# Attention with hashed masks and a SwiGLU FFN on one core: units 0 and 1 mix their heads, batch 0 is loaded in longer runs, weights are issued at other steps

## The chip, the cores and the metric

The kernel runs on one core of a Trainium2 chip. The metric is the device time of one execution in microseconds; the median of three runs of the kernel before is 370.31 us (369.69 to 371.39). A core has five engines, each with a queue of its own that it works through in order: TensorE (PE; its weight loads are listed as PEld), VectorE (DVE), ScalarE (ACT), GpSimd (POOL) and SyncE (SP). SP, ACT and POOL issue DMAs; sixteen DMA engines carry them out.

## The reference

Attention over 4 batches, 8 heads, 768 tokens, 64 dimensions. A query sees a key when the signs of their six projections agree. The output of the attention, as 3072 rows of 512, goes through an RMS norm and a gated FFN of width 1536.

```python
q_bits = (np.einsum('bhsd,dk->bhsk', q, proj) > 0)     # k likewise, 6 bits
mask = q_bucket[:, :, :, None] == k_bucket[:, :, None, :]
scores = np.where(mask, scale * q @ k.T, -1e9)
attn = np.exp(scores - max); attn = attn / (attn.sum(-1) + 1e-9)
x = (attn @ v).transpose(0, 2, 1, 3).reshape(B * S, H * D)
xn = x / np.sqrt(np.mean(x * x, -1) + 1e-6) * rms_g
g = xn @ w_gate
out = (g * sigmoid(g) * (xn @ w_val)) @ w_out
```

## The kernel before

**Units and steps.** A unit is one batch with one half of its queries (384): 8 units, `u = 2 * batch + half`. A head of a unit takes three steps; a step is two score matmuls of 128 keys x 384 queries (`scores`, L301) and one exp of 128x768 (`probs`, L313), so a unit has 24 steps (`NS`) and the kernel 192. Steps are numbered 0 to 191 here; the code writes them as a window `w` and a step `s` in it, with `at(w, s, f, ...)` entering work in `plan`. The loop at L605 emits, at each step, the scores of the next step, the exp of this one, and then all that the plan has for it. The order of every engine's queue is this order of emission: nothing is scheduled afterwards (`manual_schedule`, L60).

**The mask.** q and k of a head stand transposed in a tile `QK`, 64 rows of fp16 values and below them rows of hash bits, so that one matmul over all rows gives the score plus a large term that is highest where all six bits agree; the bias of the exp (`EBIAS`) takes it away again. Two heads (a pair, `hp`) share 12 bit rows: `select` (L212) multiplies the signs by `sel`, which keeps only the head's own six rows on the k side. With them `QK` has 76 rows (`KROWS`).

**Getting a pair ready.** Loads come into tiles of `lpool` (8 buffers). Batch 0 is turned on PE in float32 (`turn_pe`, L152: three transposes to a PSUM bank, a copy on DVE), batches 1 to 3 on DVE (`turn_dve`, L178). POOL casts the result to fp16 into `QK` (`cast_half` L170, `cast_pool` L187). The hash is a float32 matmul of the turned tile with `pj` (`hash_half`, L195), a sign on DVE (`signs`, L205) and `select`. The bits are then copied into rows 64 and up of `QK`: by DVE for the first two pairs (`hash_direct`, L218), by DMAs on SP's queue for the others (`hash_one` L234, `hash_two` L248). v is cast on POOL (`v_prep`, L267); `v_mean` (L280) gives the small constant term of the denominator's 1e-9.

**Attention out.** `av` (L318) multiplies the probabilities with v into `o_ps`, which has one PSUM buffer for a pair of heads; `attn_out` (L334) divides on DVE (`otmp`, `rcp`) and POOL (`x`, `sq`); `sumsq` reduces the squares on DVE. After the last pair of a unit comes `norm` (L364: DVE, POOL, DVE) and `turn_x` (L379).

**FFN.** `gate` (L390) and `value` (L401) work on 12 tiles of 128 columns; `project` (L415) gives the rows of the output. The FFN of unit u lies in window u+1, its projection in window u+2. The transposed tiles, hash, mean, gate, value, normed x and projection all take their PSUM bank from one pool of three (`gps`, tag "g").

**Weights.** `load_w` (L473) issues each weight matrix in two halves on POOL's queue, cast to fp16 on the way: wg at steps 3 and 7, wv at 11 and 15, wo at 30 and 34 (L531 to L534).

**Batch 0 and unit order.** In batch 0 partition p holds tokens 6p to 6p+5 (`c`). Half 0 of the queries is tokens c = 0 to 2, half 1 c = 3 to 5. A load of q or k goes to a tile `[128, 6, 2, D]` (token, head of the pair, dimension), in runs of 64 floats. Unit 0 runs all its eight heads, then unit 1 all its eight; the q half that only unit 1 needs is loaded late for pairs 0 and 1 (`qlate`). Loads of batch 1 are entered at steps 16, 20, 33 and 38, their turns at 32, 37, 43 and 48 (`spots`, L537).

Of the kernel before, what the change touches and what calls it, by code (L numbers as in the profile page):

```python
# [31 lines left out]
def kernel(  # L32
# [34 lines left out]
    pj = const.tile([128, 32], FP32, name="pj")  # L67
    sel = const.tile([128, 2], FP32, name="sel")
    ebias = const.tile([128, 1], FP32, name="ebias")
# [15 lines left out]
    def natural_tiles(hp):  # L85
        raw[0, hp] = [
            lpool.tile([128, 6, 2, D], FP32, name=n, tag="L") for n in ("qn", "kn")
        ] + [None]

    def load_natural(eng, hp, which, lo=0, hi=6):  # L90
        i = 0 if which == "q" else 1
        for hh in range(2):
            eng.dma_start(
                out=raw[0, hp][i][:, lo:hi, hh],
                in_=(q, k)[i][0, 2 * hp + hh].rearrange("(p c) d -> p c d", c=6)[:, lo:hi],
            )

    def load_v(eng, b, hp):
        vn = lpool.tile([128, 2, 6, D], FP32, name="vn", tag="L")
        for hh in range(2):  # L100
            eng.dma_start(
                out=vn[:, hh],
                in_=v[b, 2 * hp + hh].rearrange("(p c) d -> p c d", c=6),
            )
        raw[b, hp][2] = vn
# [16 lines left out]
    qlate = npool.tile([128, 2, 3, 2, D], FP32, name="qlate")  # L122
    qTlate = npool.tile([128, 2, HALF], FP32, name="qTlate")

    def load_late(eng, hp):
        for hh in range(2):
            eng.dma_start(
                out=qlate[:, hp, :, hh],
                in_=q[0, 2 * hp + hh].rearrange("(p c) d -> p c d", c=6)[:, 3:6],
            )  # L130
# [5 lines left out]
    KROWS = D + 12  # L136
    qT, kT, QK = {}, {}, {}
# [9 lines left out]
    def half_of(hp, which, half):  # L147
        if which == "q" and half == 1 and hp < 2:
            return qTlate[:, hp, :]
        return (qT if which == "q" else kT)[0, hp][:, half * HALF : (half + 1) * HALF]  # L150

    def turn_pe(hp, which, half, act=()):  # L152

        if which == "q" and half == 1 and hp < 2:
            src = qlate[:, hp]
        else:
            src = raw[0, hp][0 if which == "q" else 1][:, 3 * half : 3 * half + 3]
        src = src.rearrange("p c h d -> p c (h d)")
        ps = bank("t_ps", [128, 3, 128])
        for i in range(3):  # L160
            nc.tensor.transpose(ps[:, i, :], src[:, i], ident)  # L161
        psf = ps.rearrange("p c t -> p (c t)")
        nc.vector.tensor_copy(half_of(hp, which, half), psf)
        o = (0 if which == "q" else S) + half * HALF
        for hh in act:
            nc.scalar.copy(
                QK[0, 2 * hp + hh, "h"][0:64, o : o + HALF], psf[64 * hh : 64 * hh + 64, :]
            )

    def cast_half(hp, which, half, heads=(0, 1)):  # L170
        o = (0 if which == "q" else S) + half * HALF
        for hh in heads:
            nc.gpsimd.tensor_copy(
                QK[0, 2 * hp + hh, "h"][0:64, o : o + HALF],
                half_of(hp, which, half)[64 * hh : 64 * hh + 64, :],
            )
# [10 lines left out]
    def cast_pool(b, hp, which):  # L187
        src = (qT if which == "q" else kT)[b, hp]
# [6 lines left out]
    def hash_half(parts):  # L195

        ps = bank("d_ps", [128, HALF])
        for t, src in parts:
            nc.tensor.matmul(  # L199
                ps[32 * t : 32 * t + 32, :], pj, src,  # L200
# [17 lines left out]
    def hash_direct(n, *parts):  # L218
# [275 lines left out]
    def at(w, s, f, *a):  # L494
        if s >= NS and w < 7:
            w, s = w + 1, s - NS
# [117 lines left out]
    for s in range(NS, NS + 6):  # L614
        for f in plan[7, s]:
            f()
# [43 lines left out]
```

## Time and profile before

| what | us |
|---|---|
| median of three runs | 370.31 |
| the profiled execution | 370.79 |
| its span, first to last instruction | 369.0 |
| PE busy | 337.6 (91%) |
| DVE busy | 239.7 (65%) |
| ACT busy | 217.4 (59%) |
| POOL busy | 148.4 (40%) |
| exp (L313), 192 times | 164.8, 0.900 each |
| score matmuls (L301), 384 times | 95.9 |
| exp of step 0, 24, 48 starts at | 10.17, 46.11, 85.44 |
| exp of step 72, 96, 120, 144, 168 starts at | 130.28, 171.95, 212.20, 252.66, 291.62 |
| last exp starts at | 329.69 |

The page gives busy time by engine and by groups of instructions; a line number is a line of the kernel. The view of windows cuts the span into stretches and gives for each the busy time of every engine with the count of instructions, the granted clock of PE as a share of full speed, and the share and rate of the DMA engines. The timeline lists instructions by start and length, with the idle time before them in brackets and what ended it. The chain of waits follows the work that ended last back through what released it. In the DMA view, q0 is the queue of POOL's DMAs (the weights) and q1 that of SP's; a line gives packets, megabytes and the time that the packets took as a share of sixteen engines.

### The profile page before, as it was taken

Reading aid. Unit: us, or ns where it says so; the run is one execution under the profiler, and the core shown is the slowest. Engines: PE = TensorE matmul, PEld = TensorE weight load, DVE = VectorE, ACT = ScalarE, POOL = GpSimd, SP = SyncE. Lnnn points to the kernel's source line nnn. Section 1 sums busy time; section 2 is a strip of 40 time slices with the busy share of each in tenths; the row PEclk is TensorE's granted clock in tenths of the full one; section 3 lists DMA queues with packets and bytes.
Section 4 is the critical chain, followed back from the end, with each engine's and each line's share of the span. In section 5 each row is a group of like instructions: output and inputs, shape, how many; then the busy total and the mean of one; then the engine's idle time right before and its main releaser. Section 6 shows DMA issues by size and latency. Waiting matters only on the chain.

```text
span 369.0 us, 7544 instructions
## 1 busy us (share of the span) xinstructions
PE 337.6 (91%) x2928; PEld 199.0 (54%) x2928; DVE 239.7 (65%) x484; ACT 217.4 (59%) x316; POOL 148.4 (40%) x216
## 2 busy tenths in 40 slices
PE   7685869998989999999999999999999999998995
PEld 3452546554555645655566555555565556664552
DVE  4771748895568965986489727885566545674770
ACT  2552875654557755775667666766577667661321
POOL 3574655635513762772247522851211121112000
PEclk9986998998999999999999999999999999999999
DMA  7998699980858812004889101001100010002002
GB/s 181 213 189 180 106 180 165 167 181 20 179 105 153 170 24 80 11 3 71 169 185 187 26 30 57 3 5 25 47 30 0 2 57 30 3 0 87 0 3 85
DMA packets 100500, 31.42 MB, mean 85 GB/s; under 512 B 89968, under 2 KB 96368, under 8 KB 100464
## 3 DMA queue, kind: packets, MB, share of 16 engines
q1 hardware_dynamic: 96128, 25.82, 31.9%
q0 software_dynamic: 2656, 4.72, 7.8%
q10 hardware_dynamic: 1680, 0.40, 0.5%
q8 instruction: 23, 0.38, 0.5%
q14 instruction: 13, 0.11, 0.1%
HBM read 28.32 MB, written 6.29 MB: 94 GB/s over the span
## 4 chain that ended last, share of the span: by engine, by line
PE 75%; DVE 10%; ACT 9%; DMA 2%; issue 2%; POOL 1%; SPq 0%; DVEq 0%; ACTq 0%
PE y_ps L420 17%; PE g_ps L396 16%; PE s_ps L301 15%; PE v_ps L406 12%; PE o_ps L326 7%; ACT psb L313 7%; PE d_ps L199 4%; DMA QK<-bits 2%; ACT t L398 2%; DVE xnT L385 2%; DVE bits L214 1%; PE x_ps L384 1%; DVE kT L182 1%; PE t_ps L161 1%; DVE a L408 1%
## 5 line engine op out<-in xcount | busy, mean ns | idle before, releaser
L313 ACT ACTIVATE psb<-s_ps,ebias 128x768 f16<-128x768 f32 x192 | 164.8, 900 | 21.8 <-PE s_ps L301 21.7
L301 PE MATMUL s_ps<-QK 76*128 76x384 f16 x384 | 95.9, 332 | 15.9 <-DMA QK<-bits 6.7
L398 ACT ACTIVATE t<-g_ps 128x384 f32<-128x384 f32 x96 | 47.1, 490 | 65.3 <-PE g_ps L396 65.3
L348 POOL TENSOR_TENSOR x<-otmp,rcp 128x384 f32<-128x384 f32 x32 | 26.5, 827 | 140.0 <-DVE rcp L346 140.0
L406 PE MATMUL v_ps<-xnT,wv 128*128 128x384 f16 x384 | 78.6, 327 | 1.7 <-DVE a L408 1.6
L396 PE MATMUL g_ps<-xnT,wg 128*128 128x384 f16 x384 | 78.4, 326 | 1.1 <-DVE xnT L385 1.1
L420 PE MATMUL y_ps<-wo,ht 128*128 128x512 f16 x288 | 70.8, 380 | 0.0
L408 DVE SCALAR_TENSOR_TENSOR a<-t,g_ps 128x384 f32<-128x384 f32 x96 | 52.3, 545 | 23.4 <-ACT t L398 22.2
L301 PEld LDWEIGHTS <-QK 76*128 76x128 f16 x384 | 36.7, 99 | 52.5 <-issue 24.3
L326 PEld LDWEIGHTS <-psb 128*128 128x128 f16 x1152 | 53.2, 98 | 20.1 <-issue 4.1
L409 DVE SCALAR_TENSOR_TENSOR ht<-a,v_ps 128x384 f16<-128x384 f32 x96 | 53.2, 554 | 13.5 <-PE v_ps L406 4.7
L326 PE MATMUL o_ps<-vl,psb 128*128 128x65 f16 x1152 | 58.1, 195 | 0.5 <-ACT psb L313 0.3
L406 PEld LDWEIGHTS <-wv 128*128 128x128 f16 x384 | 34.9, 98 | 23.2 <-issue 4.1
L396 PEld LDWEIGHTS <-wg 128*128 128x128 f16 x384 | 35.1, 97 | 22.1 <-issue 1.6
L427 ACT COPY ysb<-y_ps 128x512 f32<-128x512 f32 x24 | 14.0, 585 | 55.9 <-PE y_ps L420 42.0
L420 PEld LDWEIGHTS <-ht 128*128 128x128 f16 x288 | 26.2, 98 | 25.7 <-issue 1.5
L353 POOL TENSOR_TENSOR sq<-x 128x384 f32<-128x384 f32 x32 | 26.5, 827 | 2.5
L191 POOL CAST QK<-qT 64x768 f16<-64x768 f32 x28 | 23.0, 822 | 10.5 <-DVE qT L182 8.5
L191 POOL CAST QK<-kT 64x768 f16<-64x768 f32 x28 | 23.0, 821 | 8.0 <-DVE kT L182 5.1
L341 DVE TENSOR_TENSOR otmp<-o_ps,cvb 128x390 f32<-128x390 f32 x32 | 17.8, 556 | 12.6 <-PE o_ps L326 12.3
L357 DVE TENSOR_REDUCE ssp<-sq 128x3 f32<-128x384 f32 x32 | 17.1, 534 | 10.8 <-POOL sq L353 10.7
L182 DVE STREAM_TRANSPOSE qT<-qL 128x384 f32<-128x384 f32 x24 | 20.5, 868 | 0.0
(64 smaller groups left out, 228.3 us busy)
## 6 DMA issues: line engine op xcount, KB each, us to landing
vn<-in_v_dram SPq DMA_DIRECT2D x32, 192.0 KB
out_dram<-ysb SPq DMA_DIRECT2D x24, 256.0 KB
qL<-in_q_dram SPq DMA_DIRECT2D x48, 96.0 KB
kL<-in_k_dram SPq DMA_DIRECT2D x48, 96.0 KB
wg<-in_moe_w_gate_dram POOLq DMA_DIRECT2D x2, 768.0 KB, 7.9
wv<-in_moe_w_val_dram POOLq DMA_DIRECT2D x2, 768.0 KB, 7.0
wo<-in_moe_w_out_dram POOLq DMA_DIRECT2D x2, 768.0 KB, 8.9
kn<-in_k_dram SPq DMA_DIRECT2D x6, 192.0 KB
```

Source lines behind the costliest of these rows:

```text
L191: nc.gpsimd.tensor_copy(QK[b, 2 * hp + hh, "h"][0:64, o : o + S], src[64 * hh : 64 * hh + 64, :])
L301: nc.tensor.matmul(ps[:, j, 0:HALF], QK[b, h, "h"][0:KROWS, S + jt * 128 : S + (jt + 1) * 128], QK[b, h, "h"][0:KROWS, half * HALF : (half ...
L313: nc.scalar.activation(psb[u, h][:, 2 * ch : 2 * ch + 2, :], sps.pop((u, i))[:, :, 0:HALF], AF.Exp, bias=ebias, scale=ESCALE,)
L326: nc.tensor.matmul(o[:, c, hh, 0:65], psb[u, h][:, jt, c * 128 : (c + 1) * 128], vls[b % 2][:, h, jt, 0:65], start=(hh == 0 and i == 0), s ...
L348: nc.gpsimd.tensor_mul(xd.rearrange("p c (h d) -> p c h d", h=2), tmp[:, :, :, 0:64], r.to_broadcast([128, 3, 2, 64]),)
L353: nc.gpsimd.tensor_mul(sq, xd, xd)
L396: nc.tensor.matmul(g, wg[:, kt, fs], xnT[u][:, kt, :], start=(kt == 0), stop=(kt == 3))
L398: nc.scalar.activation(t, g, AF.Tanh, scale=0.5)
L406: nc.tensor.matmul(vv, wv[:, kt, fs], xnT[u][:, kt, :], start=(kt == 0), stop=(kt == 3))
L408: nc.vector.scalar_tensor_tensor(out=a, in0=t, scalar=1.0, in1=g, op0=ALU.add, op1=ALU.mult)
L409: nc.vector.scalar_tensor_tensor(out=ht[u][:, ft, :], in0=a, scalar=0.5, in1=vv, op0=ALU.mult, op1=ALU.mult)
L420: nc.tensor.matmul(y, ht[u][:, ft, c * 128 : (c + 1) * 128], wo[:, ft, :], start=(ft == 0), stop=(ft == NF - 1),)
```

## The change

1. **Order of heads.** Steps are counted through; `order` lists (unit, head). Units 0 and 1 go: head 0 and 1 of unit 0, head 0 and 1 of unit 1, heads 2 to 7 of unit 0, heads 2 to 7 of unit 1. So pair 1 is first needed at step 12, pair 2 at 18, pair 3 at 24. From unit 2 on nothing changes in the order.
2. **Batch 0's layout.** q and k go to tiles `[128, 2, 6, D]` (head, token, dimension), in runs of 6 x 64 floats, one DMA for both heads of a pair; v too is one DMA. A transpose turns two neighbouring tokens (2 x 64 dimensions) of one head at once; the halves of the queries are the even and the odd tokens. `qlate` goes.
3. **Batch 0's hash.** The halves lie on partitions 0 to 63 and 64 to 127, so the matmul is done in two row halves (`hash_pairs`). Each head has six bit rows of its own (`KROWS0` = 70), with the k side scaled (`kscale`) in place of `select`. The two heads of pair 0 are done one after the other with DVE writing the bits into `QK` (`hash_head`); pairs 1 to 3 go by DMA (`hash_pair0`, entered at steps 6, 11 and 17).
4. **Times in the plan.** wg at steps 6 and 11, wv at 16 and 21, wo at 36 and 40. Loads of batch 1 at 21, 27, 42 and 47, turns at 30, 41, 49 and 55, each pair hashed by itself (`hash_one`). The norm of unit 0 comes at step 36, its gates and values lie in steps 40 to 47 (before: 32 to 47).

```diff
+    order = [(0, 0), (0, 1), (1, 0), (1, 1)]
+    order += [(0, h) for h in range(2, H)] + [(1, h) for h in range(2, H)]
+    order += [(u, h) for u in range(2, 8) for h in range(H)]
...
+        eng.dma_start(
+            out=raw[0, hp][i][:, h0 : h0 + n].rearrange("p h c d -> p h (c d)"),
+            in_=(q, k)[i][0, 2 * hp + h0 : 2 * hp + h0 + n].rearrange(
+                "h (p c) d -> p h (c d)", c=6
+            ),
+        )
...
+    def hash_pairs(srcs):
+        pss = [bank("d_ps", [128, HALF]) for _ in range(2)]
+        for t, src in enumerate(srcs):
+            for e in range(2):
+                nc.tensor.matmul(
+                    pss[e][32 * t : 32 * t + 32, :],
+                    pj[64 * e : 64 * e + 64, 6 * e : 6 * e + 32],
+                    src[64 * e : 64 * e + 64],
+                    start=True, stop=True, tile_position=(64 * e, 32 * t),
+                )
+        return pss
...
+    def hash_pair0(hp):
+        where = [(which, hh) for which in "kq" for hh in range(2)]
+        pss = hash_pairs([turned(hp, which)[:, hh, :] for which, hh in where])
+        bt = spool.tile([128, 2, S], FP16, name="bits")
+        for e in range(2):
+            signs(bt, pss[e], e * HALF, 128)
+        nc.vector.tensor_scalar_mul(bt[:, 0, :], bt[:, 1, :], kscale)
+        for t, (which, hh) in enumerate(where):
+            o = 0 if which == "q" else S
+            nc.sync.dma_start(
+                out=QK[0, 2 * hp + hh, "h"][64:KROWS0, o : o + S],
+                in_=bt[32 * t : 32 * t + 6, 0, :],
+            )
...
+    for hp, s0 in ((1, 3), (2, 8), (3, 14)):
+        at(0, s0, new_pair, 0, hp)
+        at(0, s0, turn_pe, hp, 0, "k")
+        at(0, s0, turn_pe, hp, 1, "k")
+        at(0, s0 + 1, cast_pool, 0, hp, "k")
+        at(0, s0 + 1, turn_pe, hp, 0, "q")
+        at(0, s0 + 2, turn_pe, hp, 1, "q")
+        at(0, s0 + 2, cast_pool, 0, hp, "q")
+        at(0, s0 + 3, hash_pair0, hp)
...
     for i in range(2):
-        at(0, 3 + 4 * i, load_w, wg, moe_w_gate, 2 * i, 2)
-        at(0, 11 + 4 * i, load_w, wv, moe_w_val, 2 * i, 2)
-        at(1, 6 + 4 * i, load_w, wo, moe_w_out, 6 * i, 6)
+        at(0, 6 + 5 * i, load_w, wg, moe_w_gate, 2 * i, 2)
+        at(0, 16 + 5 * i, load_w, wv, moe_w_val, 2 * i, 2)
+        at(0, 36 + 4 * i, load_w, wo, moe_w_out, 6 * i, 6)
...
-        1: (((0, 16), (0, 20), (1, 9), (1, 14)), ((1, 8), (1, 13), (1, 19), (2, 0))),
+        1: ((21, 27, 42, 47), (30, 41, 49, 55)),
...
     for u in range(7):
         w = u + 1
-        at(w, 5, norm, u)
+        s0, n0 = (16, 8) if u == 0 else (8, 16)
+        at(w, 12 if u == 0 else 5, norm, u)
         for c in range(3):
-            at(w, 7, turn_x, u, c)
+            at(w, 14 if u == 0 else 7, turn_x, u, c)
         for ft in range(NF):
-            at(w, 8 + (8 * ft) // 6, g_step, u, ft)
-            at(w, 8 + (8 * ft + 4) // 6, v_step, u, ft)
+            at(w, s0 + n0 * 2 * ft // 24, g_step, u, ft)
+            at(w, s0 + (2 * ft + 1) * n0 // 24, v_step, u, ft)
```

## The prediction

> **What bounds the kernel now.** First I read the windows by stage: busy time of each engine, then the granted TensorE clock (PEclk), the DMA share and GB/s.
>
> ```profile
> 13.00:24.00 11.00, 8.89 (x76) 4.81 (x75) 8.04 (x19) 6.00 (x8) 8.41 (x13) 0.84 1.02 203
> 24.00:48.00 24.00, 17.58 (x201) 11.35 (x198) 11.89 (x29) 14.67 (x19) 14.28 (x20) 0.86 0.78 149
> 48.00:87.00 39.00, 33.73 (x310) 20.57 (x307) 30.50 (x59) 24.09 (x35) 21.59 (x27) 0.93 0.93 158
> 132.00:172.00 40.00, 39.03 (x358) 22.91 (x351) 29.96 (x58) 24.89 (x38) 22.08 (x30) 1.00 0.12 31
> ```
>
> From 132 us on PE is busy 39 of 40 us: that part is PE work, and the change leaves it alone. Loss lies before 87 us. There I read the chain of waits (start, us, what) and then the timeline of the same stretch.
>
> ```profile
> 25.53 6.16 DMA QK<-bits
> 31.83 0.80 PE s_ps L301 x2
> 32.62 1.44 PE d_ps L199 x8
> ...
> 52.59 0.90 POOL rstd L374
> 53.51 1.15 DVE xn L377 x2
> 54.71 1.03 PE x_ps L384 x8
> ...
> 56.89 1.27 PE g_ps L396 x4
> ```
> ```profile
> 24.31 0.72 POOL L474 DMA_DIRECT2D wg<-in_moe_w_gate_dram  x1
> 31.83 0.80 PE L301 MATMUL s_ps<-QK 76*128 76x384 f16 x2 [4.80 <-DMA QK<-bits]
> 41.09 12.37 ACT L313 ACTIVATE psb<-s_ps,ebias 128x768 f16<-128x768 f32 x15 [0.46 <-PE s_ps L301]
> 84.86 0.54 PE L301 MATMUL s_ps<-QK 76*128 76x384 f16 x2 [1.88 <-DMA QK<-bits]
> ```
>
> PE stands 4.80 us for hash bits that travel by DMA, then works at half clock. Where nothing is missing, 15 exps take 12.37 us: 0.82 us a step. Why did 18 KB of bits take 6 us? The DMA view of 26.6 to 29.2 us, and of 56 to 60 us:
>
> ```profile
> q0 software_dynamic: 160, 0.49, 97.9%
> ...
> QK<-bits SPq DMA_DIRECT2D x2, 18.0 KB
> ```
> ```profile
> q0 software_dynamic: 613, 0.63, 101.1%
> q1 hardware_dynamic: 593, 0.08, 23.8%
> ```
>
> In the first, a weight load (queue q0) has the engines to itself though bits were issued; in the second, q0 and SP's queue q1 alternate packet for packet, whatever their size. So beside a weight load the SP queue moves nothing for about 3 us and then one packet for each weight packet. A wg or wv load runs 4.4 us, from 2.2 us after POOL issues it (wg: issued 24.31, packets 26.4 to 30.6).
>
> Anchors from the timeline (start of the exp of a step): step 0 10.17, 11 26.16, 12 32.72, 18 38.94, 24 46.11, first gate matmul 56.89, step 48 85.44. All attention of units 0 and 1 and the FFN of unit 0 lie before step 48 in both kernels, so the change is the new time of step 48.
>
> **The change, part by part.**
>
> *Runs of 1536 bytes.* q and k of batch 0 are 12288 packets of 256 bytes now and become 2048, the form of the v loads. No instruction of batch 0 but the first waits for such a load: the first transposes run at 4.56, as eight warm-up matmuls end (4.77), so that cover hides it. Worth 0; without the cover, the 4.1 us that ACT waits for qn. The 70-row score matmuls stream the same 384 columns as the 76-row ones (332 ns): 0.
>
> *First head.* One sign (0.55) and two narrow multiplies (0.25 to 0.32, as the L229 copies) replace sign, two selects (0.31 each) and two copies: step 0 at 9.4, 0.8 earlier.
>
> *Steps 3 to 11.* PE has 9 scores x 0.33 = 3.0, 8 groups of three transposes x 0.41 = 3.3, 5 half-av x 0.45 = 2.3, v_mean 0.65 and one hash. The hash has 16 instructions in two row halves; no row shows such halves. Beside each other: 0.78 (x8, at 39.50); in turn: 1.47 (x16, at 73.31). I take 1.47, the row with as many instructions. Sum 10.7, from scores(3) at 13.4: scores(12) is reached at 24.1 (before: 26.2).
>
> *Bits of pair 1, wanted by step 12.* The last copy of its turn ends at 18.0. Hash 1.5, two signs 1.1, kscale multiply 0.5 (L214 at 128x768: 507 ns): 21.1. SP issues four transfers at 0.79 (L243); step 12 needs the third: 23.5, and 1.5 to land (2.30 from issue start in the chain at 82.43): 25.0. But POOL issues the first wg right after the casts of the same pair (18.0 + 1.7), so its packets run 21.9 to 26.3, and the bits enter in the starved part. I take 26.3, step 12 at 26.7: 6.0 ahead.
>
> *Pair 2, step 18.* scores(12) comes before hash 2 on PE, so the wait is handed on. Hash at part-cold clock 2.0, signs and multiply 1.6, SP 2.4, landing 1.5: 34.4. The second wg (POOL, from unit 0's first rcp at 22.9: x and sq 1.7, casts 3.4, v_prep 0.82, then 2.2) runs 31.1 to 35.5: landing 35.5, step 18 at 36.0, 2.9 ahead.
>
> *Pair 3, step 24.* Same sum from 35.6: bits enter at 42.6; the first wv (moved to t=16; POOL, from unit 1's first rcp at 33.2: 1.7 + 3.4 + 2.2) runs 40.5 to 44.9. Landing 44.5, step 24 at 45.0, 1.1 ahead. Free of weights the three waits end at 25.0, 32 and 38.5: step 24 at 39. Blocked to the last weight packet: 47.
>
> The Trainium skill, "DMA: Bandwidth & Descriptors", section "SWDGE vs HWDGE vs iDMA", says that an engine round-robins between its queues. By that the bits would pass after one weight packet, and step 24 would be the 39 of the last lines. The view at 56 to 60 us agrees, the one at 26.6 to 29.2 does not, and the measurement decides.
>
> *Batch 1's first pair, loaded at t=21, turned at t=30.* Before, the load was issued from 38.84 and turned at 56.8, 18 us later. Now SP reaches it after the bits of pair 3 (41.5), in the middle of the two wv loads (40.5 to 49.3; POOL's second is 4.3 after its first: v_prep 0.82 twice, x, sq, issue). qL goes first, kL after; 3.45 us for four of these DMAs (L115 at 38.84) less what trickled through: kL at 54.5. Step 30 comes at 45.0 + 6 x 0.82 = 49.9. DVE waits 4 us at the head of its queue; behind it stand three transposes (0.87 each), a reduce (0.53) and otmp of unit 0's last pair (0.56), so otmp ends at 58.3. The one o_ps buffer waits for it, av of t=34 for that, and PE with it.
>
> *The norm of unit 0.* rcp 0.2, x and sq 1.7, and POOL's queue then holds two casts (1.7), a v_prep (0.82) and the wo issue (0.93) ahead of ms and rstd (1.1): 64.7. xn 1.5, last transposes and xnT 1.0: first gate 66.9, ten later than before, but with 40 steps of attention done instead of 33. Without DVE's wait: 64.
>
> *Steps 40 to 48.* FFN 0 now in 8 steps: 96 matmuls x 0.163 (0.65 for four) = 15.6, 8 x (0.33 + 0.30) = 5.0, one hash 0.8: 21.4, and 0.6 for DVE, which has 12 x (545 + 554) + 4 x 870 + some 2.5 = 19.2 in that stretch. Step 48 at 88.9, that is +3.5.
>
> *After step 48.* Half clock at 85.2 to 88.6 follows PE's 1.88 us wait for batch 1's bits (84.86). These bits now leave 13 steps ahead: the 1.7 us of half clock go. Four hash_one for two hash_two cost the same matmuls.
>
> Sum: 3.5 - 1.7 = +1.8 us on this execution's 369.0 span (370.79 with what lies around it). Against the median, 370.31 + 1.8 = **372.1 us**. Its own range is +/-4: step 24 from 41 to 47.
>
> **The rivals.**
>
> *Bits pass between weight packets (ends faster).* For it: equal packet counts at 56 to 60 us. Against: none at 26.6 to 29.2. It needs the bits to land within 2 us of issue in two of the three cases. Then step 24 is at 39 to 41. The wv loads also start some 4 earlier, kL lands near 50, otmp at 53.8, first gate 62.4, step 48 at 84.4: -1.0 - 1.7 = -2.7. If kL also shares its engines and DVE never waits, the gate is at 58 and step 48 at 80: -7. I put it at 365.
>
> *DVE and the three PSUM buffers bound steps 40 to 48 (slower).* 19.2 us of DVE work in 22, with 870 ns transposes between the `a` and `ht` operations that free the buffers. If PE waits out each of four transposes and half of eight exps (0.45): 3.5 + 3.6 less the 0.6 counted: +6.5, 378.
>
> *Nothing is gained or lost:* the head order only shifts waits. Half of the pieces above cancel, and that would be 370.3.
>
> **How the numbers follow.** A measurement of this kernel tells about 0.5% (1.85 us) from no change. Forecast 0.50 (slower 0.29, same 0.13, faster 0.08), passing bits 0.31 (faster 0.28, same 0.03), DVE 0.16 (slower), nothing 0.03. Together faster 0.36, same 0.19, slower 0.45. Range 362 to 379; the forecast's own is 368 to 376.
>
> **What would show it.** Right: PE waits of 1 to 4 us for QK<-bits before steps 12, 18 and 24; step 24 near 45; DVE's first L173 transpose of batch 1 waiting for kL some 4 us; first gate near 67; steps 40 to 48 in 22 us; no half clock after step 48. Wrong: step 24 before 42, or that transpose not waiting (the faster rival), or over 25 us for steps 40 to 48 (the DVE rival). A changed time for steps 72 to 191 or for the tail would say that something else happened.

## The result, and the profile after

| | before | after |
|---|---|---|
| median, us | 370.75 (369.69 to 371.39, 4 runs) | 382.32 (379.84 to 383.53, 4 runs) |
| the profiled execution, its span | 370.79, 369.0 | 383.31, 381.5 |
| exp of step 0, 12, 24 starts at | 10.2, 32.7, 46.1 | 8.8, 29.8, 44.9 |
| exp of step 36, 48 | 62.9, 85.4 | 62.7, 94.7 |
| first gate matmul of unit 0 | 56.9 | 71.8 |
| exp of step 72, 96, 191 | 130.3, 172.0, 329.7 | 141.7, 184.8, 342.3 |
| half clock granted, within the span | 17.6 | 42.6 |

The ratio is 1.031, with a 95% interval of 1.024 to 1.037: slower, by 11.6 us. Medians, here and below, are of all runs; ratios and their intervals are of the fast runs alone. The changed kernel is 1.2 us ahead at step 24, 1.8 behind at step 30, level at step 36 and 9.3 us behind at step 48. Another 3.6 us go by step 96: 3.9 are gained by step 55, 3.1 are lost again just ahead of step 56, 2.9 in steps 56 to 72 and 1.4 in 72 to 96. From there on the two run alike.

The windows of the changed kernel, columns as before (length, then busy time of PE, its weight loads, DVE, ACT and POOL, then PEclk, DMA share, GB/s):

```profile
13.00:24.00 11.00, 10.01 (x107) 7.61 (x108) 7.44 (x17) 7.37 (x10) 4.78 (x6) 0.84 0.17 32
24.00:48.00 24.00, 16.83 (x185) 10.25 (x180) 9.26 (x21) 13.46 (x16) 15.88 (x20) 0.80 0.64 129
48.00:72.00 24.00, 17.30 (x147) 10.22 (x148) 11.17 (x23) 12.07 (x14) 11.11 (x15) 0.64 0.91 165
72.00:95.00 23.00, 22.61 (x165) 12.86 (x164) 17.06 (x33) 11.62 (x20) 6.38 (x8) 0.91 0.56 97
```

Between 13 and 24 us the transfer engines, full before (1.02), are used to 0.17: batch 0's loads are nearly over by then (SP's queue takes 6.0% of the engines' time there, 64.9% before), and the weights come later (10.9%, 36.5% before). From 24 to 72 us no engine is busy for three quarters of the time, and PE has a mean clock of 0.80 and then 0.64. From 72 to 95 us PE is busy throughout: it makes up for the FFN of unit 0. The chain of waits names what stood still:

```profile
23.61 5.12 DMA QK<-bits
28.87 0.80 PE s_ps L325 x2
...
43.01 5.69 DMA QK<-bits
48.84 0.81 PE s_ps L325 x2
...
55.32 2.80 DMA kL<-in_k_dram
...
59.84 0.83 POOL QK L186
60.72 0.83 POOL QK L186
61.65 0.84 POOL x L372
...
67.10 0.90 POOL rstd L398
68.02 1.28 DVE xn L401 x3
69.99 1.77 DVE xnT L409 x3
71.81 1.44 PE g_ps L420 x4
```

The first line answers to the 6.16 us of before; now there is a second such wait, for the second head of pair 3. The scores that wait for it are those of step 27, not 24: three of pair 3's four transfers entered from 42.2 to 43.8 us, just ahead of the first wv packet (43.8), and only the fourth was caught behind the weights. Then the late k of batch 1 holds DVE, and POOL casts that k ahead of x, so that rstd of unit 0 starts 14.5 us and the first gate 14.9 us later than before. The list of waits (time in all, times, longest) shows what each cost its engine:

```profile
PE s_ps L325 <- DMA QK<-bits: 6.3, 2, 4.6
PE o_ps L350 <- DVE otmp L365: 3.8, 1, 3.8
DVE kT L173 <- DMA kL<-in_k_dram: 3.5, 1, 3.5
```

Why is k late? SP's timeline (start, length, count of DMAs):

```profile
32.75 10.92 SPq L249 DMA_DIRECT2D QK<-bits  x8
43.77 5.48 SPq L116 DMA_DIRECT2D qL<-in_q_dram  x4
49.35 6.61 SPq L116 DMA_DIRECT2D kL<-in_k_dram  x4
```

SP is at the bits of pairs 2 and 3 for 10.9 us: eight issues of 0.7 us, and between them, from 35.7 to 40.9, a wait, for it works in order and those of pair 3 aren't there yet. q and k of batch 1 are behind them. And while the first bits travel, the DMA view of 24 to 26.5 us has the weights alone, as before:

```profile
q0 software_dynamic: 163, 0.50, 103.7%
...
QK<-bits SPq DMA_DIRECT2D x2, 9.0 KB
```

After step 48 the place to look at is unit 1's norm. On POOL four casts of batch 1's third pair stand between sq and ms, and on DVE (second timeline) that pair's bits, a cvb and a transpose of the fourth pair stand between xn and xnT:

```profile
100.88 0.83 POOL L377 TENSOR_TENSOR sq<-x 128x384 f32<-128x384 f32 x1
101.64 1.70 POOL L186 CAST QK<-kT 64x768 f16<-64x768 f32 x2
103.41 1.71 POOL L186 CAST QK<-qT 64x768 f16<-64x768 f32 x2
105.21 0.20 POOL L394 TENSOR_SCALAR ms<-ss 128x3 f32<-128x3 f32 x1
```
```profile
106.40 1.82 DVE L401 TENSOR_SCALAR xn<-x,rstd 128x512 f16<-128x512 f32 x3 [3.91 <-POOL rstd L398]
108.14 0.54 DVE L202 TENSOR_SCALAR bits<-d_ps 128x384 f16<-128x384 f32 x1
108.72 0.68 DVE L209 TENSOR_SCALAR bits<-bits,sel 128x384 f16<-128x384 f16 x2
109.31 0.28 DVE L312 TENSOR_SCALAR cvb<-m_ps 128x130 f32<-128x130 f32 x1
109.52 0.85 DVE L173 STREAM_TRANSPOSE kT<-kL 128x384 f32<-128x384 f32 x1
110.22 2.03 DVE L409 TENSOR_TENSOR xnT<-x_ps,gcol 128x512 f16<-128x512 f16 x3
```

The casts do not make the difference to the kernel before: from the reciprocal of unit 1's last pair to rstd's end 6.5 us pass, where the kernel before took 7.8, since there ms waited for a hash on PE and its signs. From rstd's end to unit 1's first gate 7.8 us pass instead of 4.8, and half clock begins at 110.3. These 3.0 us fit the 3.1 that go just ahead of step 56.

**An account of step 48.** The records of PE laid over the stretches of granted clock split the time up to step 48 into the matmuls at full speed, half of PE's busy time under half clock (what the low clock added), and idle time. The ends of matmuls are modelled, so this is good to about half a microsecond.

| kernel | step 48 | at full speed | added by half clock | idle |
|---|---|---|---|---|
| before | 85.4 | 61.5 | 6.2 | 17.8 |
| after | 94.7 | 60.5 | 14.9 | 19.4 |

So the 9.3 us look like 8.7 of clock and 1.6 of idle time, less 1.0 of work. This account tells where the time shows, not what would bring it back; the experiments had to say that.

### The profile page after: what moved, and what is told of

It is laid out like the page before. It is cut to its first block, busy times and chain, and to the rows that moved or that the text cites. A ratio compares the mean times of both kernels' runs of the same rounds, so it can differ in the third digit from the quotient of the medians.

```text
span 381.5 us, 7588 instructions
## 1 busy us (share of the span) xinstructions
PE 346.5 (91%) x2956; PEld 202.9 (53%) x2956; DVE 237.5 (62%) x475; ACT 218.1 (57%) x315; POOL 148.3 (39%) x215
## 3 DMA queue, kind: packets, MB, share of 16 engines
q1 hardware_dynamic: 86960, 25.98, 29.5%
## 4 chain that ended last, share of the span: by engine, by line
PE 70%; DVE 9%; ACT 7%; POOL 6%; DMA 4%; issue 2%; SPq 2%; DVEq 0%; ACTq 0%; POOLq 0%
PE g_ps L420 16%; PE y_ps L444 14%; PE s_ps L325 13%; PE v_ps L430 13%; PE o_ps L350 7%; ACT psb L337 5%; DMA QK<-bits 3%; POOL QK L186 2%; ACT t L422 2%; DVE xnT L409 2%; PE d_ps L219 2%; PE d_ps L194 2%; SPq L116 1%; PE t_ps L148 1%; DVE bits L202 1%
## 5 line engine op out<-in xcount | busy, mean ns | idle before, releaser
L325 PE MATMUL s_ps<-QK 76*128 76x384 f16 (+1 forms) x384 | 100.1, 345 | 14.0 <-DMA QK<-bits 6.3
L372 POOL TENSOR_TENSOR x<-otmp,rcp 128x384 f32<-128x384 f32 x32 | 26.5, 829 | 142.9 <-DVE rcp L370 142.7
L420 PE MATMUL g_ps<-xnT,wg 128*128 128x384 f16 x384 | 80.0, 331 | 1.2 <-DVE xnT L409 1.1
L350 PEld LDWEIGHTS <-psb 128*128 128x128 f16 x1152 | 55.1, 101 | 28.8 <-issue 15.1
L350 PE MATMUL o_ps<-vl,psb 128*128 128x65 f16 x1152 | 60.0, 198 | 5.5 <-DVE otmp L365 3.8
L325 PEld LDWEIGHTS <-QK 76*128 76x128 f16 (+1 forms) x384 | 37.4, 102 | 49.9 <-issue 18.4
L420 PEld LDWEIGHTS <-wg 128*128 128x128 f16 x384 | 35.6, 98 | 23.7 <-issue 3.6
L186 POOL CAST QK<-kT 64x768 f16<-64x768 f32 x24 | 19.7, 821 | 25.9 <-DVE kT L173 16.5
L377 POOL TENSOR_TENSOR sq<-x 128x384 f32<-128x384 f32 x32 | 26.5, 827 | 2.5
L365 DVE TENSOR_TENSOR otmp<-o_ps,cvb 128x390 f32<-128x390 f32 x32 | 17.8, 556 | 15.4 <-PE o_ps L350 15.4
L186 POOL CAST QK<-qT 64x768 f16<-64x768 f32 x24 | 19.8, 823 | 9.5 <-DVE qT L173 8.7
L202 DVE TENSOR_SCALAR bits<-d_ps 128x384 f16<-128x384 f32 (+1 forms) x22 | 11.9, 554 | 17.8 <-PE d_ps L219 10.2
L173 DVE STREAM_TRANSPOSE kT<-kL 128x384 f32<-128x384 f32 x24 | 20.5, 865 | 3.5 <-DMA kL<-in_k_dram 3.5
```

Of the source, the lines that this page charges most:

```text
L186: nc.gpsimd.tensor_copy(QK[b, 2 * hp + hh, "h"][0:64, o : o + S], src[64 * hh : 64 * hh + 64, :])
L325: nc.tensor.matmul(ps[:, j, 0:HALF], QK[b, h, "h"][0:rows, S + jt * 128 : S + (jt + 1) * 128], QK[b, h, "h"][0:rows, half * HALF : (half + ...
L350: nc.tensor.matmul(o[:, c, hh, 0:65], psb[u, h][:, jt, c * 128 : (c + 1) * 128], vls[b % 2][:, h, jt if b else 2 * (jt % 3) + jt // 3, 0:6 ...
L372: nc.gpsimd.tensor_mul(xd.rearrange("p c (h d) -> p c h d", h=2), tmp[:, :, :, 0:64], r.to_broadcast([128, 3, 2, 64]),)
L377: nc.gpsimd.tensor_mul(sq, xd, xd)
L420: nc.tensor.matmul(g, wg[:, kt, fs], xnT[u][:, kt, :], start=(kt == 0), stop=(kt == 3))
```

## The experiments

Medians of three or five rounds; "step 24" means the start of its exp in the profiled execution. The kernel before ran beside each, at 369.9 to 371.9 us.

**One wait at a time.** In the lists `1: (loads, turns)` are batch 1's steps.

```diff
-        1: ((21, 27, 42, 47), (30, 41, 49, 55)),
+        1: ((12, 27, 42, 47), (30, 41, 49, 55)),
```


> The changed kernel with batch 1's first pair loaded at step 12 instead of 21; nothing else differs. Theory Q (kL comes late behind the wv loads; DVE stands at its first transpose, POOL's casts of that pair stand for DVE, and x, sq, ms and rstd of unit 0's norm stand behind these casts): kL lands before step 30, DVE and POOL do not wait, the first gate comes at 64 to 66 us instead of 71.8 and the time falls from 382 to 375-377. Rival D (the loss is the FFN of unit 0 packed into 8 steps, and half clock): the first gate may move but the time stays at 380-383.

383.0 us (ratio 1.033, 1.023 to 1.042). DVE's wait for k is gone, but the bits wait 5.2 us at step 12 and 5.3 at step 24 (50.6), and the first gate is at 71.4. The wait moved to the bits.

```diff
+        1: ((21, 27, 42, 47), (36, 41, 49, 55)),
```


> The changed kernel with batch 1's first pair turned from step 36 instead of 30; its load stays at 21. Q: DVE and POOL reach the late pair only after unit 0's last otmp, x and norm, so the first gate comes at 63 to 66 us and the time falls to 374-376, though kL lands as late as before. If the late load itself were the limit and not what is queued behind it, the time stays at 380-383. D: 380-383 too.

380.0 us (1.023, 1.016 to 1.031). First gate 69.8, step 48 at 95.1; the gain, if it is one, is within the intervals, with the bits' waits at 5.3 and 4.2 us.

```diff
-        at(0, 6 + 5 * i, load_w, wg, moe_w_gate, 2 * i, 2)
-        at(0, 16 + 5 * i, load_w, wv, moe_w_val, 2 * i, 2)
-        at(0, 36 + 4 * i, load_w, wo, moe_w_out, 6 * i, 6)
+        at(0, 3 + 4 * i, load_w, wg, moe_w_gate, 2 * i, 2)
+        at(0, 11 + 4 * i, load_w, wv, moe_w_val, 2 * i, 2)
+        at(0, 30 + 4 * i, load_w, wo, moe_w_out, 6 * i, 6)
```


> The changed kernel with the weights issued at the steps of the kernel before (wg 3 and 7, wv 11 and 15, wo 30 and 34). Theory W (the later weights are what the change loses by): 370-374. Q: the last wv load ends 3 to 4 us earlier and kL with it, so part of the DVE wait goes: 377-380. If the loads only change places with the bits: 381-384.

379.0 us (1.018, 1.008 to 1.029; its runs lie between 377.0 and 382.9). Step 24 at 48.9, first gate 71.1, step 48 at 92.1; half clock from 44.2 to 71.5 without a break.

The next run keeps layout, runs and row-halved hash, but has the old order of heads with its plan times, and pair 1's bits by DVE as in the kernel before:

```diff
-    order = [(0, 0), (0, 1), (1, 0), (1, 1)]
-    order += [(0, h) for h in range(2, H)] + [(1, h) for h in range(2, H)]
-    order += [(u, h) for u in range(2, 8) for h in range(H)]
+    order = [(u, h) for u in range(8) for h in range(H)]
```


> The changed kernel with the order of heads and the plan's times of the kernel before (units 0 and 1 one after the other, FFN of unit 0 over steps 32 to 47, weights and batch 1's loads as before, pair 1's bits written by DVE); what stays is the new layout, its longer runs, the row-halved hash and the pair-wise hash of batch 1. If the layout costs nothing: 367-372, like the kernel before. If the layout is what costs: 376 or more.

372.7 us (1.005, 1.001 to 1.010). What this kernel keeps of the change costs about 2 us; the order of heads, with its plan times and pair 1's bits by DMA, the other 9.6. The 2 us are not the layout's alone: the diff of the change also moved batch 2's loads and its first two turns (61 and 67 to 66 and 72), which the list of the change leaves out, this run keeps them, and its steps 72 to 96 take 43.1 us for 41.7.

**Weights out of the bits' way.**

```diff
+        at(0, 19 + i, load_w, wg, moe_w_gate, 2 * i, 2)
+        at(0, 26 + 2 * i, load_w, wv, moe_w_val, 2 * i, 2)
+        1: ((12, 27, 42, 47), (30, 41, 49, 55)),
```


> The changed kernel with batch 1's first q and k loaded at unit 1's step 12 instead of 21, the gate weights issued at unit 0's steps 19 and 20 and the value weights at 26 and 28 (before: 6, 11, 16, 21). Now no weights lie beside the bits of a pair. Theory B (what costs is that a weights load holds the transfer engines while the 9 KB of bits stand behind it, and then the late k): the bits waits of 6.3 us at steps 12 and 24 fall under 2 us, so step 12 at 25.5 us from the span's start (29.8 in the changed kernel), step 24 at 40 (44.9), the first gate at 62 (71.8), step 48 at 84 to 87 (94.7), and the time is 371 to 374 us. Rival C (what costs is the clock, which is at half when TensorE has little to do, whatever empties it): steps 12 and 24 come early, but the half clock in 24 to 76 us stays above 20 us and steps 36 to 48 need 28 us and more, so that the time stays at 378 us or above.

378.9 us (1.022, 1.016 to 1.028). Half of it came true. PE's timeline around steps 12 and 24:

```profile
25.52 0.48 PE L325 MATMUL s_ps<-QK 70*128 70x384 f16 x2 [1.36 <-DMA QK<-bits]
46.17 0.80 PE L325 MATMUL s_ps<-QK 70*128 70x384 f16 x2 [7.93 <-DMA QK<-bits]
```

Without weights beside them the first bits are waited for 1.36 us and step 12 comes at 26.1, as expected. The weights, issued later, now run into the bits of pair 3, and all is given back there: step 24 at 47.1.

Then without any transfer of weights, in both kernels (the weight tiles hold a constant that VectorE sets, so the FFN's results differ):

```diff
     def load_w(dst, src, kt, n):
-        nc.gpsimd.dma_start(
-            out=dst[:, kt : kt + n, :],
-            in_=src[kt * 128 : (kt + n) * 128, :].rearrange("(k p) n -> p k n", p=128),
-        )
+        if dst is not wg:
+            nc.vector.memset(dst[:, kt : kt + n, :], 0.01)
+    nc.vector.memset(wg, 0.01)
```


> The changed kernel without its 9.4 MB of weights: the three weight tiles are set to 0.01 by VectorE (the gate weights ahead of step 0, the halves of the other two at steps 16, 21, 36 and 40, some 1.6 us each) and no transfer is made for them, so the FFN's results differ. Theory D (the weights' transfers are what delays the bits and the late k, and with them everything up to step 48): the bits waits fall under 1.5 us together, step 24 comes at 36 to 38 us (44.9), the first gate at 54 to 58 us (71.8), and the time at 362 to 368 us, no more than 2 us from the kernel before without weights. Rival P (the mixed order itself: unit 0's FFN has only steps 40 to 47 for its 24 pairs of gate and value, its norm stands behind POOL's casts, and TensorE has nothing else to do until then): step 24 comes early as well, but the time stays 6 us or more above that of the kernel before without weights.

> The kernel before without its weights' transfers, in the same way; the mate of the run ahead of it. Its first gate at 56.9 us came 5.8 us after its last score of unit 0's FFN inputs, and its bits waits were 2 to 4 us. Theory D: it gains less than the changed kernel, 364 to 368 us. Rival P: it gains as much or more, 358 to 366 us, and the distance to the changed kernel without weights stays at 6 us and above.

380.7 us (1.022, 1.015 to 1.030) and 375.9 us (1.012, 1.007 to 1.018). As a measure of the whole these two failed: the memsets of a half took 2.62 us instead of 1.6, the one of wg ahead of step 0 took 5.18 and delayed step 0 to 12.6 us, and two of them stand in the changed kernel's chain. What they do show is the bits (PE's timeline of the changed kernel without weights):

```profile
31.08 0.48 PE L325 MATMUL s_ps<-QK 70*128 70x384 f16 x2 [1.43 <-DMA QK<-bits]
46.04 0.80 PE L325 MATMUL s_ps<-QK 70*128 70x384 f16 x2 [1.61 <-DMA QK<-bits]
```

Both waits, ahead of steps 12 and 24, fall to 1.5 us. The distance of the two kernels, 4.8 us, lies between the two expectations (2 and 6), so it settles nothing between them.

**The norm alone.**

```diff
+        1: ((12, 27, 42, 47), (39, 43, 49, 55)),
```


> The changed kernel with batch 1's first q and k loaded at step 12 instead of 21, and the turns of its first two pairs at steps 39 and 43 instead of 30 and 41, so that neither VectorE's transposes nor GpSimd's casts of batch 1 stand ahead of unit 0's norm (step 36). Theory N (those casts and the transposes waiting for the late k delay unit 0's norm by some 8 us, which the prediction left out): the first gate comes 4 us after step 38, at 66 us or before (71.8), step 48 at 88 to 90 (94.7), and the time at 375 to 378 us. Rival: the norm comes early, but the turns then stand in steps 39 to 47, where the FFN of unit 0 needs VectorE for each of its 24 products: step 48 stays at 93 us and above, and the time at 380 us and above.

381.3 us (1.028, 1.021 to 1.034). Step 40 comes at 68.1 (70.6) and the gate 1.7 us behind it (1.2), but the bits' waits (5.0 and 5.2 us, step 24 at 50.8) had eaten the gain before: gate 69.8, step 48 at 91.7.

**The clock.** Matmuls of zeros that nobody reads:

```diff
+    FILL = {(0, i): 3 for i in range(6, 24)}
+    FILL.update({(1, i): 3 for i in range(6, 18)})
+    FILL[0, 6] = FILL[0, 18] = 40
...
+        for _ in range(FILL.get((u, i), 0)):
+            nc.tensor.matmul(
+                ps[:, 0, HALF:512], zeros16[:, 0:128], zeros16[:, 0:128], start=True, stop=True
+            )
```


> The changed kernel plus matmuls of zeros that nobody reads (128 rows into 128 unused columns of the score bank): three in each of steps 6 to 41 of the mixed units, 40 ahead of the scores of step 12 and 40 ahead of those of step 24, where TensorE waits for the bits. All waits stay. Theory C (the half clock is the cost): the half clock between 24 and 76 us falls from 23.8 us to under 10 us, and the time to 373 to 377 us. Rival B (the waits are the cost, the half clock follows from them and costs little): the half clock falls as well or not, and the time stays at 380 us or above, since the fillers add some 3 to 8 us of TensorE's own time.

378.1 us (1.023, 1.017 to 1.030), between the two. In the account of step 48 (92.1): half clock adds 5.0 instead of 14.9 and idle time is 17.1, but full-speed work is 70.0 instead of 60.5. The fillers spent on PE nearly all that the clock gave, so this doesn't price the clock.

```diff
+    FILL = {(0, 12): 40, (2, 0): 16}
...
+    at(1, 7, warm, 1, 8)
```


> The kernel before with such zero matmuls where its TensorE stands idle: 40 ahead of the scores of step 12, 16 ahead of those of step 24, 32 just ahead of unit 0's transposes of x. Theory C: the 19.6 us of half clock of the kernel before shrink to under 12 us and the time falls to 365 to 368 us. If half clock falls there on time that waits for something else anyway: 370 to 371 us. If the fillers stand in the way: 372 us and above.

369.5 us (0.999, 0.995 to 1.002): no difference. (The second group stood ahead of step 48, not 24, and of the 19.6 us of half clock 2.0 lie past the span's end.) Up to step 48 PE's time under half clock stayed as it was, and idle time turned into fillers.

> The kernel with the new layout but the heads in the old order, plus 40 zero matmuls ahead of the scores of step 12, where its TensorE waited 4.42 us for bits and where its one stretch of half clock (30.7 us from 31.7 us on) began. If that stretch was a cost (TensorE was busy for 11.5 of the 12 us between 48 and 60 us, at half clock): it shrinks to 10 us or less and the time falls from 372.7 to 366 to 369 us, under both kernels. If the half clock falls on time in which something else is waited for: 371 us and above.

372.9 us (1.006, 1.003 to 1.009), against 372.7 without fillers. This tells more: half clock up to step 48 added 7.2 us instead of 14.5, and step 48 moved by 0.3 us only, 88.8 to 88.5. The fillers were 4.0 us of work and idle time rose by 3.0. Where PE runs slow beside a wait that would end no earlier, a faster PE only waits longer.

```diff
+    FILL = {(0, 6): 80, (0, 18): 80}
...
+    at(1, 14, warm, 1, 15, 24)
+    at(2, 7, warm, 2, 8, 36)
```


> The changed kernel with batch 1's first loads at step 12, plus zero matmuls only where TensorE waits there: 80 ahead of the scores of step 12 and 80 ahead of those of step 24 (4.3 us each, the waits were 5.2 and 5.3 us), 24 ahead of unit 0's transposes of x and 36 ahead of unit 1's. None stand elsewhere. Theory C (each wait costs twice, once as idle time and once as the half clock that follows): TensorE's busy time at half clock up to step 48 falls from 24.1 us to under 10, step 48 comes at 85 to 88 us (92.3), and the time at 374 to 378 us (383.0). Rival: the half clock falls, but other waits take its place, and step 48 stays at 91 us or later, the time at 380 us or above.

381.1 us (1.025, 1.020 to 1.030). PE's timeline at step 24:

```profile
44.84 4.63 PE L326 MATMUL s_ps<-zeros 128*128 128x128 f16 x80
54.10 0.80 PE L331 MATMUL s_ps<-QK 70*128 70x384 f16 x2 [4.63 <-DMA QK<-bits]
```

After 4.63 us of fillers PE still waits 4.63 us, and the clock falls to half at 51.8 all the same. Filling the waits is no cure. The execution shown took 386.3 us and the other three 379.0 to 381.3, so only these waits are read from it.

**The bits another way.** VectorE writes them to their rows; no transfer is made, and the return leaves out the multiply by `kscale` and the four DMAs behind it. This stands on the first edit above (loads at step 12):

```diff
         for e in range(2):
             signs(bt, pss[e], e * HALF, 128)
+        for t, (which, hh) in enumerate(where):
+            o = 0 if which == "q" else S
+            nc.vector.tensor_scalar_mul(
+                QK[0, 2 * hp + hh, "h"][64:KROWS0, o : o + S],
+                bt[32 * t : 32 * t + 6, 1, :], 4.0 * BIT * BIT if which == "k" else 1.0,
+            )
+        return
         nc.vector.tensor_scalar_mul(bt[:, 0, :], bt[:, 1, :], kscale)
         for t, (which, hh) in enumerate(where):
```


> The same base (first loads at step 12), and the bits of pairs 1 to 3 are written to their rows by VectorE (four instructions of some 0.3 us a pair) instead of by four transfers of 9 KB. No weights can stand ahead of them now. Theory B+C: the waits of 5.2 and 5.3 us at steps 12 and 24 fall to 1 to 2 us, step 12 comes at 26 us, step 24 at 39 to 41 us, half clock up to step 48 falls under 12 us, step 48 at 83 to 87 us, and the time at 373 to 377 us. Rival P (unit 0's FFN within steps 40 to 47 sets the time, whatever comes before): step 24 early, first gate still at 67 us or later, 380 us or above.

375.0 us (1.005, 1.000 to 1.010), from 383.0 (1.033). Step 12 at 27.1, gate 64.1, step 48 at 85.1: near the first expectation, but for step 24 (43.7 for 39 to 41) and the half clock up to step 48 (17.1 us, not under 12). VectorE's writes took up to 0.88 us each instead of 0.3.

> The changed kernel with one edit alone: VectorE writes the bits of pairs 1 to 3 to their rows, and no transfer does. Loads, weights and turns are those of the change. If the bits' way is the main cause: 374 to 376 us, as with the early loads (375.0); q and k of batch 1's first pair are still loaded at step 21, but SP no longer stands blocked behind the bits, so that they come some 5 us earlier. If the late k and the casts ahead of the norm weigh as much: 378 us and above.

375.3 us (1.015, 1.011 to 1.019), from 382.3 (1.031). By the medians one edit alone brings 7.0 of the 11.6 us; by the ratios to the kernel before beside each, half of the loss. SP's timeline with it:

```profile
19.19 3.54 SPq L116 DMA_DIRECT2D qL<-in_q_dram  x4
22.82 6.86 SPq L116 DMA_DIRECT2D kL<-in_k_dram  x4
```

With no bits to stand at, SP issues batch 1's k from 22.8 us (49.4), and DVE's wait for it is gone too. The chain between steps 12 and 24:

```profile
30.03 0.87 DVE QK L248
30.92 0.88 DVE QK L248
...
33.44 0.48 DVE otmp L372
```

DVE's writes are on the chain now, in place of 5 us waits (k's wait was 0 here). Step 48 is level with the kernel before (85.5 and 85.4); the remaining 4.7 us of span lie in steps 48 to 96.

Next, on the run with the bits by VectorE and the loads at step 12 (375.0 us), the weights issued early, as in the third edit above, and the turns clear of the norm:

```diff
+        1: ((12, 27, 42, 47), (39, 43, 49, 55)),
```


> The run before, with the weights issued early as well (gate at steps 3 and 7, value at 11 and 15, out at 30 and 34) and the turns of batch 1's first two pairs at steps 39 and 43, so that nothing of batch 1 stands ahead of unit 0's norm. If the parts add up: step 24 at 38 to 40 us, first gate at 60 to 63 us, step 48 at 81 to 84 us, and the time at 368 to 372 us, the best of the mixed order. If the turns beside the FFN of unit 0, or steps 56 to 96, take it back: 374 us or above.

369.7 us (0.996, 0.992 to 0.999). Step 24 at 42.5, gate 59.1, step 48 at 81.0. What could not show while the bits blocked adds up now. Steps 72 to 96 still take 43.2 us.

```diff
-        2: ((56, 62, 68, 74), (66, 72, 80, 86)),
+        2: ((52, 56, 63, 68), (61, 67, 80, 86)),
```


> The best mixed version so far (bits by VectorE, early weights, first two turns of batch 1 at steps 39 and 43: 369.7 us) with the loads and turns of batch 2 put back to the steps of the kernel before (loads 52, 56, 63, 68 for 56, 62, 68, 74; turns 61, 67, 80, 86 for 66, 72, 80, 86). If the later turns of batch 2 are what steps 72 to 96 lost: 41.7 us there instead of 43.1, and 368 us. If the lost time only moves to steps 56 to 72, where the last turn of batch 1 stands: 369.5 us and above.

371.0 us (0.994, 0.990 to 0.998), not to be told from the run before this edit (0.996). In the profile steps 72 to 96 take 42.4 us, 0.8 less than there, and steps 48 to 72 take 47.7 (44.9): the time did not go away.

**Is it the mix?** The same edit in the kernel before, for its pairs 2 and 3:

```diff
-            nc.sync.dma_start(
-                out=QK[0, hp][64:KROWS, :, o : o + HALF],
-                in_=bt[32 * t : 32 * t + 12, :, 0:HALF],
-            )
+            for hh in range(2):
+                nc.vector.tensor_copy(
+                    QK[0, hp][64:KROWS, hh, o : o + HALF],
+                    bt[32 * t : 32 * t + 12, hh, 0:HALF],
+                )
```


> The kernel before, with the bits of pairs 2 and 3 of batch 0 copied to their rows by VectorE (eight copies of some 0.3 us a pair) instead of sent by four transfers a pair. If the transfers of the bits cost there what they cost in the mix: its two waits of 6.7 us together fall to 2, and the time to 365 to 368 us. If VectorE's 2.4 us a pair or the next wait (its first gate stands behind the late transposes) takes the gain: 369.5 us and above.

366.4 us (0.986, 0.982 to 0.990): faster than both kernels, and its six runs lie within 0.7 us. Step 12 at 29.5, step 24 at 44.4, gate 55.2, step 48 at 82.7.

> The new layout with the heads in the old order (372.7 us), and the bits of pairs 2 and 3 by VectorE as well. If the old order gains as the mix does: 366 to 369 us, and then the mix itself has brought nothing beside the best mixed version's 369.7. If the old order is bounded elsewhere: 371 us and above, and then the mix is worth 2 us or more once the bits go another way.

369.0 us (0.994, 0.991 to 0.997). With the bits off the queue the new layout stands at 0.994 in the old order and at 0.994 in the best mix, on the same chip; the old layout in the old order stands at 0.986. Part of that last distance may again be batch 2's moved turns, which the first of the three keeps (steps 72 to 96: 43.1 us for 41.7). The mixed order brought nothing that could be measured.

| kernel | step 48 | at full speed | added by half clock | idle |
|---|---|---|---|---|
| after, bits by VectorE | 85.5 | 63.1 | 6.4 | 15.9 |
| the same, weights and turns moved | 81.0 | 62.2 | 5.0 | 13.8 |
| before, bits by VectorE | 82.7 | 62.7 | 5.1 | 14.9 |

Taking the waits away lowered the idle time and what the half clock adds together, at 1.2 to 2.6 us more work on PE's account.

## Why the prediction was wrong

It said 372.1 us, with 362 to 379; it is 382.3. The direction of the likeliest case, slower, was right, and the size was not. Of the 10.7 us by which the profiled execution exceeds the forecast sum (12.5 against 1.8), 5.8 had gathered by step 48 and 4.9 came after it.

- **Runs, first head, steps 3 to 11: held.** Step 0 at 8.8 (9.4); PE reached the scores of step 12 at 24.2 (24.1). The hash in row halves took 0.94 us for 16 matmuls, not 1.47; the halves run beside each other.
- **The three waits for bits: the first step that failed.** Pair 1's bits landed at 28.7 (26.3), since wg's packets ran from 22.8 to 27.7 (21.9 to 26.3) and the first packet of bits moved at 26.7; step 12 came at 29.8 (26.7), after a wait of 4.6 us. Before step 18 there was no wait for bits; it came at 37.8 (36.0) since step 12 was late. The gain there was put against a wrong anchor: 38.94 is step 16 of the kernel before, step 18 starts at 41.1. Step 24 at 44.9 (45.0) was luck: wv started 3.3 us later than forecast (43.8 for 40.5), so the bits that step 24 needs passed ahead of it, and the wait of 1.7 us fell on step 27. That the SP queue is starved beside a weight load was the right reading: 163 packets of weights and none of SP's in the window from 24 us above, and waits of 1.5 us without weights. The round-robin of the Trainium skill ("DMA: Bandwidth & Descriptors", "SWDGE vs HWDGE vs iDMA") does not show there packet by packet; what an engine takes as one turn no run here tells. The range of 41 to 47 for step 24 was too narrow: the first three experiments have 48.9 to 50.6.
- **Batch 1's k: later by 3.6 us.** The forecast had SP reach qL at 41.5, after the bits of pair 3, and k landed at 54.5. Its own terms (35.6, hash 2.0, signs and multiply 1.6, four issues of 0.79) make 42.4 for SP. SP reached qL at 43.8, and k landed at 58.1, 14.3 us later (13.0 forecast); SP was at the issue of qL and kL for 12.1 us of them. The wait of DVE, 3.5 us, is as foretold (4), but only because step 30 was late too: 52.7 for 49.9, with 7.8 us for six steps that the forecast had at 0.82 each, the clock at half from 45.4 to 55.7. So otmp ended at 61.3 (58.3).
- **The norm of unit 0: mis-sized by 1.9 us.** From otmp's end to the first gate 10.5 us (8.6). The queue of POOL was summed rightly (6.4; 6.7 to rstd's end), but normalizing, transposes and copies ran to 3.8 us instead of 2.2, where the forecast's own 1.5 and 1.0 make 2.5; the clock was at half from 69.3. Gate 71.8 for 66.9.
- **Steps 40 to 48: held.** From the first gate to step 48 22.9 us for 22.0. PE was busy for 22.6 of the 23 us from 72 on, so VectorE did not bound them, and the slower rival came about neither there nor through its mechanism.
- **After step 48: the sign was wrong, and terms were left at nothing.** The forecast took 1.7 us of half clock back and cost the rest at nothing; the profile has +3.2. With batch 1's turns moved, that batch's bits and transposes stood on DVE between rstd and unit 1's first gate, 7.8 us for 4.8, and half clock followed from 110.3 to 117.1. Steps 56 to 72 lost 2.9 us, 1.6 of them by step 58. Steps 72 to 96 lost 1.4, and nothing in the forecast had counted the turns of batch 2 that were moved; it held that the change left alone all from 132 us on. They take 43.1 us in the three kernels that have the old order of heads but these turns, 41.7 in the kernel before with its bits by VectorE, and 42.4 in the mix with the old turns.
- **The half clock: left out.** Within the span it went from 17.6 to 42.6 us. The forecast cost each wait as idle time, took a slow hash into pair 2's sum, and gave the clock one refund. By the account the half clock added 8.7 us more up to step 48 than in the kernel before.
- **The passing-bits rival (365 us)** came near on step 48, and its result was far off: with no bits on the queue step 24 comes at 42.7 and step 48 at 85.5 (it said 39 to 41 and 84.4), but the time is 375.3, as what lies behind step 48 is lost in that case too.

What is shown, by one edit in each of four kernels: the bits' way through SP's queue costs 7.0 us by the medians and 5.7 by the ratios in the changed kernel, 8.1 and 10.3 with early loads, 3.7 and 4.2 in the old order with the new layout, and 4.8 and 5.3 in the kernel before. It covers the starved packets, SP's standing at them, and the late k behind. In the changed kernel it is the whole loss up to step 48 (85.5 without it, 85.4 before the change) and about half of the loss in all. The other half lies behind step 48: the run with early loads, early weights and other turn times makes up for it (0.996), mostly ahead of step 48, which it reaches at 81.0 us instead of 85.4; which of these edits does it, and which of the turns' new times costs what in steps 48 to 96, stays open. What is only argued: that the low clock is a second price of each wait. The fillers showed that raising the clock alone brings little or nothing; no run separated the clock from the wait that caused it.

## What to carry to other kernels

A few kilobytes that an engine could write in 2 to 4 us should not travel on an in-order queue beside loads of hundreds of kilobytes: here they waited for packets ahead of them, and everything issued behind them waited for their producer. When a wait has several causes in a row, removing one can show little (383.0, 380.0, 379.0, 378.9 here, from 382.3), so look for the one resource that all of them share. And test a new order of work against the old one with the same obstacle removed: here the order that started two units early brought nothing that the old order did not have too.

## What the runs showed that was not expected

- SP's issue of four loads of 96 KB took from 2.63 us to 11.54 us (the longest while wg and wv travelled, in the run with the weights after the bits): the issuing queue itself stands still, and so does all that is behind it.
- PE's clock fell to half after a wait of 1.6 us (12.2 to 13.8, half from 14.7, in the changed kernel) as in ones of 5, and stayed there for 3.4 to 30.7 us at a time, in stretches that are whole multiples of 3.41 us. The longest, from 31.7 to 62.4 us in the new layout with the old order, went on although PE was busy for 29.0 of the 30.0 us from 32.4 on.
- VectorE's four writes of 6 x 768 fp16 elements took 1.56 us for pair 1 and 3.54 us for pair 2, in the changed kernel with the bits by VectorE. POOL had no cast beside the first and two casts and a v_prep beside the second, as its timelines show (VectorE's, then POOL's):

```profile
21.74 1.56 DVE L248 TENSOR_SCALAR QK<-bits 6x768 f16<-6x768 f16 x4
28.26 3.54 DVE L248 TENSOR_SCALAR QK<-bits 6x768 f16<-6x768 f16 x4
```
```profile
21.47 0.94 POOL L503 DMA_DIRECT2D wg<-in_moe_w_gate_dram  x1
...
27.20 1.70 POOL L164 CAST QK<-kT 64x768 f16<-64x768 f32 x2
28.96 0.83 POOL L300 CAST vl<-vn 128x768 f16<-128x768 f32 x1
29.75 1.84 POOL L164 CAST QK<-qT 64x768 f16<-64x768 f32 x2
```

That the casts are the cause is an inference; the same two writes took 1.71 and 3.55 us in the best mixed version's profile, beside the same work.
